# A decode step with attention over a long cache, gated with an MLP: halves of three large loads, P times V's rows summed on DVE, wo in other packets and behind the last V

## The chip, the cores and the metric

The kernel runs on one core of a Trainium2 chip. The core has a matrix engine (PE, with a queue of its own for loading weights, PEld), a vector engine (DVE), a scalar engine (ACT), GpSimd (POOL) and a sync engine (SP), which work side by side and wait for each other by semaphores. PE writes to PSUM, a small accumulation memory; everything else lies in SBUF, 128 partitions. 16 DMA engines move data between HBM and SBUF; a transfer is issued by an instruction on an engine's queue, here almost always SP's, and SP works through its queue in order.

The metric is device time in microseconds, the median of several executions.

## What is computed

Two sequences (B = 2), one new token each. One branch is attention with 32 heads of 128 over a cache of 16384 keys and values per head; the other is a small MLP; a scalar gate mixes them. Cut to what matters:

```python
def reference(A_x, A_k_cache, A_v_cache, A_wq, A_wo, B_x, B_w1, B_w2, B_w3, B_w4, gate_w):
    g = sigmoid((x * gate_w).sum(-1, keepdims=True))        # x = A_x, (2, 1, 1024)
    # attention, H = 32, Dh = 128, Sk = 16384
    q = (x @ wq).reshape(B, 1, H, Dh).transpose(0, 2, 1, 3)
    p = softmax(einsum("bhqd,bhkd->bhqk", q, k_cache) * Dh ** -0.5)
    a = einsum("bhqk,bhkd->bhqd", p, v_cache).transpose(0, 2, 1, 3).reshape(B, 1, H * Dh) @ wo
    # MLP, F = 3584
    h = gelu(layernorm(x) @ w1)
    hs = shift(h) @ w2                # with one token the four shifted quarters are zeros
    x1 = x + hs
    b = x1 + gelu(layernorm(x1) @ w3) @ w4
    return g * a + (1 - g) * b
```

All data are bfloat16. The two caches are 268 MB each, wq and wo 8.4 MB each, w3 and w4 7.3 MB each, w1 and w2 2.1 MB each.

## The kernel before

**Units.** The work on the cache is cut into 32 units: a unit is a pair of heads (`hp`, 16 of them) of one sequence (`b`). Its K is 8.4 MB, 64 KB in each partition: partition p holds 256 consecutive rows of 128 numbers, and the first 64 partitions are one head, the others the second. Its V has the same form.

**Memory.** `mem` has five cells of 32 KB per partition; a K or V takes two. K of even units lies in cells 0 and 1, K of odd units in 1 and 2, so that the next K may start to load when half of the present one has been used (each unit begins with the half that lies in cell 1). V lies in cells 3 and 4, but for unit 30, whose V takes cells 0 and 1 when K is no longer needed there. At the start wq lies in cells 3 and 4, w1 and w2 in cell 2; then w3 and after it w4 take cells 3 and 4, and then the first V.

**A unit n** (the loop at line 567): `score_first` and `score_second` work through K in 8 chunks of 32 rows per partition. DVE transposes a chunk (L425, two buffers), and PE multiplies it by q (L431, 8 products per chunk), which builds the scores S in PSUM. Between the two halves stands the issue of the next K (L97). `softmax_a` transposes S (L452), takes the maximum of each partition (L454) and spreads it on a diagonal (L456, ACT). `softmax_b` has PE bring the maxima together (L462), DVE reduces them (L468), ACT takes the exponentials (L470) with their sums, and a product and a reciprocal give the inverse row sums (L481, L483). P times V of a unit comes two units later: `pv(n - 2)` (L503) makes 64 products into `oacc`, in which 32 rows hold partial results (8 in each of four groups of columns of PE, each with four blocks of 128). `pv_end` scales and copies `oacc` on ACT (L516), and four fp32 products with selecting weights (L521, two records each) add the rows that belong together into O, transposed; L533 multiplies by the gate. After the second sequence of a pair, `wo_project` (L404) multiplies by the pair's two heads of wo: four products of 512 columns into the output sum `arow`, which lies in PSUM in two halves of 512 columns, each in its own group of PE's columns.

**Order.** A scheduler builds each engine's queue nearly in the program's order. SP's queue in a middle unit is: K of the next unit (waits for DVE's transposes of half of this one), V of the unit before (waits for the last P-times-V product that reads cells 3 and 4), and in every fourth unit a load of wo for four heads (`load_wo`, 1 MB, rows of 2 KB, one buffer).

**The MLP** is spread over the first units. `LinearT` (line 197) loads a weight matrix whole and multiplies 128x128 blocks of it by two columns of activations (L217). w3's 224 products run in unit 0 behind S, 56 of them ahead of the softmax's maximum product, 168 behind the product for the row sums; then the gelu follows on DVE and ACT. w4's 224 run in unit 1 in the same way. `lin4.load` waits for the last product that reads w3; `load_v(0)` waits for the last that reads w4. `mlp_post4` starts the output sum with 16 fp32 products (L379).

**The end.** V of unit 31 comes in 11 pieces (`PIECES`, in rows per partition: six of 32, three of 16, two of 8), each issued ahead of its use. The first three go through `pv_moving`; the rows of the others are used as weights against P (L548) as they arrive, into the same sum. Behind V stand two loads of one head of wo each. Then the last `wo_project`, a copy of each half of `arow` (L606 on DVE, L608 on ACT), and one store per half.

## Time and profile before

| | |
|---|---|
| runs of the kernel (us) | 1347.13, 1347.13, 1348.85; median 1347.13 |
| the profiled execution | 1348.32, its span 1346.6 |
| mean granted clock of PE | 0.781 |
| read from HBM | 572.53 MB, 425 GB/s over the span |
| busy, share of the span | PE 59%, DVE 48%, PEld 27%, ACT 9%, POOL 1% |
| largest groups | S products L431 547.9 us, K transposes L425 570.8 us, P times V L503 116.9 us |

The profile is one execution. "Busy" is the time in which an engine had an instruction of that group under way; a matrix product of fp32 has two records. The chain that ended last follows the work back from the last instruction to what released it. A wait is put down to the event that came last. The arrival of a transfer is the moment at which its semaphore was seen; the DMA columns of the windows count its packets, which is earlier. Every line number in a profile line is a line of the kernel it belongs to.

### The profile page before, as it was taken

Reading aid. Unit: us, or ns where it says so; the run is one execution under the profiler, and the core shown is the slowest. Engines: PE = TensorE matmul, PEld = TensorE weight load, DVE = VectorE, ACT = ScalarE, POOL = GpSimd, SP = SyncE. Lnnn points to the kernel's source line nnn. Section 1 sums busy time; section 2 is a strip of 40 time slices with the busy share of each in tenths; the row PEclk is TensorE's granted clock in tenths of the full one; section 3 lists DMA queues with packets and bytes.
Section 4 is the critical chain, followed back from the end, with each engine's and each line's share of the span. In section 5 each row is a group of like instructions: output and inputs, shape, how many; then the busy total and the mean of one; then the engine's idle time right before and its main releaser. Section 6 shows DMA issues by size and latency. Waiting matters only on the chain.

```text
span 1346.6 us, 12381 instructions
## 1 busy us (share of the span) xinstructions
PE 790.9 (59%) x5542; PEld 367.0 (27%) x5542; DVE 644.4 (48%) x503; ACT 127.1 (9%) x197; POOL 15.2 (1%) x54
## 2 busy tenths in 40 slices
PE   2678765554766545566555556655456664555665
PEld 2455322222222222222222222222222222222222
DVE  0434555444555534455554345555344555444450
ACT  0010101111110011110011111001111100111110
POOL 1000000000000000000000000000000000000000
PEclk9967877777887667888777788777778876777886
DMA  9988999999999999999999999999999999999997
GB/s 406 432 368 387 435 436 427 425 429 437 433 431 433 428 439 435 433 433 425 433 433 435 435 435 435 435 432 426 437 437 425 429 433 437 433 433 429 435 435 303
DMA packets 16109, 573.33 MB, mean 426 GB/s; under 512 B 1844, under 2 KB 1848, under 8 KB 6584
## 3 DMA queue, kind: packets, MB, share of 16 engines
q1 hardware_dynamic: 16052, 572.54, 98.8%
q8 instruction: 43, 0.70, 0.2%
q14 instruction: 10, 0.08, 0.0%
q10 hardware_dynamic: 4, 0.00, 0.0%
HBM read 572.53 MB, written 0.00 MB: 425 GB/s over the span
## 4 chain that ended last, share of the span: by engine, by line
DMA 66%; PE 16%; DVE 12%; issue 4%; ACT 0%; another core or an unknown queue 0%; POOL 0%; SPq 0%; DVEq 0%; ACTq 0%
DMA mem<-in_A_k_cache_dram 62%; PE S L431 12%; DVE KT L425 12%; DMA mem<-in_A_v_cache_dram 3%; PE misc L217 3%; DMA xin<-in_A_x_dram 2%; PE misc L248 1%; ACT pt L470 0%; PE arow L379 0%; PE oacc L503 0%; POOL ln_rstd L329 0%; PE misc L462 0%; PE arow L404 0%; PE misc L481 0%
## 5 line engine op out<-in xcount | busy, mean ns | idle before, releaser
L431 PE MATMUL S<-KT,qw 128*128 128x512 bf16 x2048 | 547.9, 418 | 388.4 <-DVE KT L425 388.2
L425 DVE STREAM_TRANSPOSE KT<-mem 128x2048 f32<-128x2048 f32 x256 | 570.8, 2282 | 297.3 <-DMA mem<-in_A_k_cache_dram 245.8
L431 PEld LDWEIGHTS <-qw 128*128 128x128 bf16 x2048 | 219.0, 107 | 712.2 <-issue 533.8
L503 PE MATMUL oacc<-mem,pt 128*8 128x512 bf16 x2008 | 116.9, 386 | 8.7 <-DMA mem<-in_A_v_cache_dram 8.7
L456 ACT ACTIVATE Dm<-ident_s,m 128x128 f32<-128x128 f32 x32 | 12.9, 402 | 1018.4 <-DVE m L454 1018.4
L470 ACT ACTIVATE pt<-St,nb 64x256 bf16<-64x256 f32 x64 | 89.7, 1401 | 58.4 <-DVE nb L468 57.5
L533 DVE TENSOR_SCALAR OT<-misc,g_rep 128x2 bf16<-128x2 f32 x31 | 6.9, 222 | 143.5 <-PE misc L521 143.5
L481 PE MATMUL misc<-rs,lmat 128*128 128x1 f32 x62 | 18.2, 362 | 90.0 <-ACT pt L470 90.0
L503 PEld LDWEIGHTS <-pt 128*8 128x8 bf16 x2008 | 46.7, 87 | 75.7 <-issue 25.3
L452 DVE STREAM_TRANSPOSE St<-S 128x512 f32<-128x512 f32 x32 | 22.9, 717 | 66.2 <-PE S L431 66.2
L483 DVE RECIPROCAL rinv<-misc 128x1 f32<-128x1 f32 x31 | 5.2, 169 | 102.2 <-PE misc L481 102.2
L521 PE MATMUL misc<-sel,osb 128*128 128x2 f32 x256 | 33.7, 254 | 27.1 <-ACT osb L516 27.1
L481 PEld LDWEIGHTS misc<-rs,lmat 128*128 128x128 f32 x62 | 15.5, 311 | 101.2 <-ACT pt L470 101.2
L521 PEld LDWEIGHTS misc<-sel,osb 128*128 128x128 f32 x256 | 31.0, 191 | 43.3 <-ACT osb L516 43.3
L217 PEld LDWEIGHTS <-mem 128*128 128x128 bf16 x576 | 36.3, 170 | 1.8 <-issue 1.4
L470 ACT ACTIVATION_READ_ACCUMULATOR pt<-St,nb 64x1 f32 x64 | 30.5, 477 | 0.0
L516 ACT ACTIVATE osb<-oacc,rinv 128x512 f32<-128x512 f32 x31 | 21.3, 687 | 72.6 <-PE oacc L503 72.6
L248 PE MATMUL misc<-xT,mem 128*128 128x2 bf16 x256 | 7.1, 165 | 26.1 <-DVE xT L243 23.3
L280 POOL TENSOR_TENSOR qw<-qd,mask 128x16 bf16<-128x16 bf16 x32 | 8.4, 265 | 1195.2 <-PE S L431 1166.6
L468 DVE TENSOR_REDUCE nb<-misc 64x1 f32<-64x64 f32 x64 | 14.2, 222 | 5.3 <-PE misc L462 1.3
L224 DVE COPY w_acc<-misc 128x16 f32<-128x16 f32 (+4 forms) x6 | 1.1, 176 | 31.4 <-PE misc L217 31.4
L462 PE MATMUL misc<-Dm,ones_f 128*128 128x128 f32 x64 | 15.8, 331 | 0.0
(83 smaller groups left out, 124.3 us busy)
## 6 DMA issues: line engine op xcount, KB each, us to landing
mem<-in_B_w_dram SPq DMA_DIRECT2D x2, 7168.0 KB, 29.1
wo<-in_A_wo_dram SPq DMA_DIRECT2D x7, 1024.0 KB, 33.0
mem<-in_A_v_cache_dram SPq DMA_DIRECT2D x6, 1024.0 KB, 24.1
mem<-in_B_w_dram SPq DMA_DIRECT2D x2, 2048.0 KB
mem<-in_A_v_cache_dram SPq DMA_DIRECT2D x3, 512.0 KB, 16.7
mem<-in_A_k_cache_dram SPq DMA_DIRECT2D x32, 28.3
wo<-in_A_wo_dram SPq DMA_DIRECT2D x1, 512.0 KB, 32.0
mem<-in_A_v_cache_dram SPq DMA_DIRECT2D x2, 256.0 KB, 13.3
```

What stands on the lines that cost most here:

```text
L217: nc.tensor.matmul(ps[:, c - c0, :], lhsT=wc[:, r, :].rearrange("p (m c) -> p c m", c=self.C)[:, c, :], rhs=self.actT[:, r, :], start=(r = ...
L248: nc.tensor.matmul(qps[:, h, :], lhsT=wq_t[:, r, h * Dh : (h + 1) * Dh], rhs=xT[:, r, :], start=(r == 0), stop=(r == KC - 1),)
L425: nc.vector.transpose(out=kt[:], in_=Kc.rearrange("p j d -> p (j d)").bitcast(FP32))
L431: nc.tensor.matmul(S, lhsT=t[:, v, NG - 1 - m : NG - 1 - m + P], rhs=ktb[:, half * GT : (half + 1) * GT, w, :, e], start=(first and n == 0 ...
L452: nc.vector.transpose(out=st[:].rearrange("p j r -> p (j r)"), in_=S[:])
L462: nc.tensor.matmul(R_ps[:], lhsT=ones_f[:], rhs=Dm[:], start=True, stop=True)
L468: nc.vector.tensor_reduce(out=nb[rows], in_=R_ps[rows, rows], axis=AX.X, op=ALU.min)
L470: nc.scalar.activation(out=Pt[rows, :, e, :].rearrange("p (m a) k -> p a k m", a=GT // 4), in_=st[rows, :, 0:NG].rearrange("p (a k) m -> p ...
L481: nc.tensor.matmul(tot_ps[:, 0:1], lhsT=lmat[:], rhs=rs[:], start=True, stop=True)
L503: nc.tensor.matmul(acc[QP * q : QP * q + 8, :], lhsT=pts[u % NP][:, g].rearrange("p h k -> p (h k)"), rhs=v_view(u)[:, 4 * g : 4 * g + 4, ...
L516: nc.scalar.activation(out=osb[:], in_=oacc[u % 2][:], func=ACTF.Copy, scale=rinvs[u % NP][:, 0:1] if scaled else 1.0,)
L521: nc.tensor.matmul(ot[:], lhsT=osb[:, k * Dh : (k + 1) * Dh], rhs=sel8[:, k : k + 5 : 4], start=(k == 0), stop=(last and k == 3),)
```

## The change

- `LinearT` may load its matrix in parts, each with half of the rows of every partition, in a cell of its own; `compute` works on a part, and the second part's result is added to the first's on DVE. w3 and w4 have two parts (cells 3 and 4). `lin4.load(0)` stands behind the products on the first half of w3, `lin4.load(1)` behind those on the second; the two halves of the first V (`load_v_half`) follow the halves of w4 in the same way.
- `softmax_b` is cut in two; the row sums become `softmax_c`, so that an issue can stand between them.
- `pv_end` and `pv_last`: the rows of `oacc` are weighted by a mask (which carries the inverse row sum and the gate) and added over the four blocks on DVE (`pv_rows`), and one or two fp32 products with a selector of the head replace the four. The ACT copy goes.
- wo is loaded for pairs of heads with rows of 4 KB, two consecutive rows of wo in each partition; O is laid out to fit, even and odd rows apart. The last four heads, not the last two, are loaded one by one behind the last V, and projected at the end.
- The output sum lies in four groups of columns of PE, 256 numbers each, in one tile (cleared once at the start). `wo_project` makes 8 products of 256 columns, `mlp_post4` 32 of 32 columns. At the end DVE copies one half of each group and ACT the other, and there is one store per sequence.
- `PIECES` is seven of 32 and two of 16.

```diff
         nc.sync.dma_start(out=region(v_cell[u], NJ * Dh), in_=cache_rows(A_v_cache, u))
-    PIECES = [32] * 6 + [16] * 3 + [8] * 2
+    def load_v_half(u, k):
+        at = slice(k * CELL, (k + 1) * CELL)
+        nc.sync.dma_start(out=region(v_cell[u], NJ * Dh)[:, at], in_=cache_rows(A_v_cache, u)[:, at])
+    PIECES = [32] * 7 + [16] * 2
     assert sum(PIECES) == NJ
...
     )
+    mask4m = const.tile([P, 4], FP32)
+    nc.vector.tensor_tensor(out=mask4m[:], in0=sel8[:, 0:4], in1=sel8[:, 4:8], op=ALU.add)
+    hsel = const.tile([P, 2], FP32)
+    nc.vector.tensor_reduce(
+        out=hsel[:], in_=sel8[:].rearrange("p (h k) -> p h k", k=4), axis=AX.X, op=ALU.add
+    )
     oacc = [ops.tile([P, 4 * Dh], FP32, name=f"oacc{k}") for k in range(2)]
...
     class LinearT:
-        def __init__(self, W, actT, name, cell, offset):
+        def __init__(self, W, actT, name, cell, offset, nparts=1):
             self.actT = actT
...
             self.C = self.N // P
+            self.rows = self.R // nparts
             self.src = W.rearrange("(p r) n -> p (r n)", p=P)
-            at = cell * CELL + offset
-            self.dst = mem[:, at : at + self.R * self.N]
+            self.at = [(cell + k) * CELL + offset for k in range(nparts)]
             self.acc = mlp.tile([P, self.C, B], FP32, name=f"{name}_acc")
-        def load(self):
-            nc.sync.dma_start(out=self.dst, in_=self.src)
-        def compute(self, c0, c1):
-            wc = self.dst.rearrange("p (r n) -> p r n", n=self.N)
+        def part(self, k):
+            return mem[:, self.at[k] : self.at[k] + self.rows * self.N]
+        def load(self, k=0):
+            n = self.rows * self.N
+            nc.sync.dma_start(out=self.part(k), in_=self.src[:, k * n : (k + 1) * n])
+        def compute(self, k, c0, c1):
+            wc = self.part(k).rearrange("p (r n) -> p r n", n=self.N)
             ps = misc_psum([P, c1 - c0, B])
             for c in range(c0, c1):
-                for r in range(self.R):
+                for r in range(self.rows):
                     nc.tensor.matmul(
...
                         lhsT=wc[:, r, :].rearrange("p (m c) -> p c m", c=self.C)[:, c, :],
-                        rhs=self.actT[:, r, :],
+                        rhs=self.actT[:, k * self.rows + r, :],
                         start=(r == 0),
-                        stop=(r == self.R - 1),
+                        stop=(r == self.rows - 1),
                     )
-            nc.vector.tensor_copy(out=self.acc[:, c0:c1, :], in_=ps[:])
+            acc = self.acc[:, c0:c1, :]
+            if k == 0:
+                nc.vector.tensor_copy(out=acc, in_=ps[:])
+            else:
+                nc.vector.tensor_tensor(out=acc, in0=acc, in1=ps[:], op=ALU.add)
     xn1T = mlp.tile([P, KC, B], BF16)
...
     lin2 = LinearT(B_w2, shT, "w2", 2, KC * D)
-    lin3 = LinearT(B_w3, xn2T, "w3", 3, 0)
-    lin4 = LinearT(B_w4, h2T, "w4", 3, 0)
+    lin3 = LinearT(B_w3, xn2T, "w3", 3, 0, 2)
+    lin4 = LinearT(B_w4, h2T, "w4", 3, 0, 2)
     lin1.load()
...
             )
-    lin3.load()
+    lin3.load(0)
+    lin3.load(1)
     qT = const.tile([P, H, B], BF16)
...
         layernorm_T(x1T[:], xn2T[:], "ln2")
-    NH2 = D // 512
-    arow_t = [rps.tile([QP * k + B, 512], FP32, name=f"arow{k}") for k in range(NH2)]
-    arow = [arow_t[k][QP * k : QP * k + B, :] for k in range(NH2)]
+    NQ = D // Q4
+    arow_t = rps.tile([P, NQ], FP32, name="arow")
+    nc.vector.memset(arow_t[:], 0.0)
+    arow = [arow_t[QP * k : QP * k + B, :] for k in range(Q4)]
     def mlp_post4():
...
         )
-        W = 512 // KC
-        for k in range(NH2):
+        W = NQ // KC
+        for k in range(Q4):
             for c in range(KC):
...
                 )
-    OT = const.tile([P, H, B], BF16)
-    WOH = 4
-    wo_view = A_wo.rearrange("(h d) n -> d h n", d=Dh)
+    OT = const.tile([P, HP, 2, B], BF16)
+    LASTP = 2
+    wo_pairs = A_wo.rearrange("(hp p r) n -> p hp (r n)", p=P, r=2)
+    wo_heads = A_wo.rearrange("(h d) n -> d h n", d=Dh)
     wo_tiles = {}
-    def load_wo(h0, n, step=WOH):
-        t = wopool.tile([P, WOH, D], BF16, name="wo")
-        for k in range(0, n, step):
-            z = min(n, k + step)
-            nc.sync.dma_start(out=t[:, k:z, :], in_=wo_view[:, h0 + k : h0 + z, :])
-        for k in range(n):
-            wo_tiles[h0 + k] = t[:, k, :]
+    def wo_tile(hp0):
+        t = wopool.tile([P, 2, 2, D], BF16, name="wo")
+        for k in range(2):
+            for r in range(2):
+                wo_tiles[hp0 + k, r] = t[:, k, r, :]
+        return t
+    def load_wo_pair(hp0):
+        t = wo_tile(hp0)
+        nc.sync.dma_start(
+            out=t[:].rearrange("p k r n -> p k (r n)"), in_=wo_pairs[:, hp0 : hp0 + 2, :]
+        )
+    def load_wo_last():
+        t = wo_tile(HP - LASTP)
+        for k in range(2):
+            for r in range(2):
+                nc.sync.dma_start(out=t[:, k, r, :], in_=wo_heads[:, H - 4 + 2 * k + r, :])
     def wo_project(hp):
-        for h in (2 * hp, 2 * hp + 1):
-            for k in range(NH2):
+        for r in range(2):
+            for k in range(Q4):
                 nc.tensor.matmul(
                     arow[k],
-                    lhsT=OT[:, h, :],
-                    rhs=wo_tiles[h][:, k * 512 : (k + 1) * 512],
+                    lhsT=OT[:, hp, r, :],
+                    rhs=wo_tiles[hp, r][:, k * NQ : (k + 1) * NQ],
                     start=False,
-                    stop=(h == H - 1),
+                    stop=(hp == HP - 1 and r == 1),
                     skip_group_check=True,
...
         rs_tiles[u] = rs
+    def softmax_c(u):
+        rs = rs_tiles.pop(u)
         tot_ps = misc_psum([P, 2])
...
         pv_moving(u, 0, NJ // 4, NJ // 4)
-    def pv_sum(u, ot, scaled, last):
-        osb = ppool.tile([P, 4 * Dh], FP32, name="osb")
-        nc.scalar.activation(
-            out=osb[:], in_=oacc[u % 2][:], func=ACTF.Copy,
-            scale=rinvs[u % NP][:, 0:1] if scaled else 1.0,
-        )
-        for k in range(4):
-            nc.tensor.matmul(
-                ot[:],
-                lhsT=osb[:, k * Dh : (k + 1) * Dh],
-                rhs=sel8[:, k : k + 5 : 4],
-                start=(k == 0),
-                stop=(last and k == 3),
-            )
+    def pv_rows(u, mask):
+        acc = oacc[u % 2]
+        part = ppool.tile([P, Dh], FP32, name="part")
+        red = ppool.tile([P, 2, Dh], FP32, name="red")
+        nc.vector.tensor_scalar(
+            out=part[:], in0=acc[:, 0:Dh], scalar1=mask[:, 0:1], scalar2=None, op0=ALU.mult
+        )
+        for k in range(1, 4):
+            in0 = acc[:, k * Dh : (k + 1) * Dh]
+            twice = k == 3
+            nc.vector.scalar_tensor_tensor(
+                out=red[:] if twice else part[:],
+                in0=in0.unsqueeze(1).to_broadcast([P, 2, Dh]) if twice else in0,
+                scalar=mask[:, k : k + 1],
+                in1=part[:].unsqueeze(1).to_broadcast([P, 2, Dh]) if twice else part[:],
+                op0=ALU.mult,
+                op1=ALU.add,
+            )
+        return red[:].rearrange("p e d -> p (e d)")
     def pv_end(u):
         hp, b = units[u]
-        ot = misc_psum([P, 2])
-        pv_sum(u, ot, True, True)
+        mask = stat.tile([P, 4], FP32, name="maskr")
         nc.vector.tensor_scalar(
-            out=OT[:, 2 * hp : 2 * hp + 2, b], in0=ot[:], scalar1=g_rep[:, b : b + 1],
-            scalar2=None, op0=ALU.mult,
-        )
+            out=mask[:], in0=mask4m[:], scalar1=rinvs[u % NP][:, 0:1],
+            scalar2=g_rep[:, b : b + 1], op0=ALU.mult, op1=ALU.mult,
+        )
+        red = pv_rows(u, mask)
+        if hp >= HP - LASTP:
+            ot = misc_psum([P, 2])
+            nc.tensor.matmul(ot[:], lhsT=red[:, 0:Dh], rhs=hsel[:], start=True, stop=True)
+            nc.vector.tensor_copy(out=OT[:, hp, :, b], in_=ot[:])
+            return
+        ot = misc_psum([P, 2, 2])
+        for r in range(2):
+            nc.tensor.matmul(
+                ot[:, r, :],
+                lhsT=red[:, r : 2 * Dh : 2],
+                rhs=hsel[:],
+                start=True,
+                stop=True,
+            )
+        for e in range(2):
+            rows = slice(e * HALF, (e + 1) * HALF)
+            nc.vector.tensor_copy(out=OT[rows, hp, :, b], in_=ot[rows, :, e])
         if b == B - 1:
...
         pv_moving(u, 0, moving, moving)
-        pv_sum(u, ot, False, False)
+        red = pv_rows(u, mask4m)
+        nc.tensor.matmul(ot[:], lhsT=red[:, 0:Dh], rhs=hsel[:], start=True, stop=False)
         V = v_view(u)
...
             )
-        nc.vector.tensor_tensor(
-            out=OT[:, 2 * hp : 2 * hp + 2, b], in0=ot[:], in1=rinvs[u % NP][:], op=ALU.mult
-        )
-        wo_project(hp)
+        nc.vector.tensor_tensor(out=OT[:, hp, :, b], in0=ot[:], in1=rinvs[u % NP][:], op=ALU.mult)
+        for k in range(HP - LASTP, HP):
+            wo_project(k)
     compute_gate()
     layernorm_T(xT[:], xn1T[:], "ln1")
-    lin1.compute(0, lin1.C)
+    lin1.compute(0, 0, lin1.C)
     mlp_post1()
-    lin2.compute(0, lin2.C)
+    lin2.compute(0, 0, lin2.C)
     mlp_post2()
...
         if n == 0:
-            lin3.compute(0, FC // 4)
+            load_wo_pair(0)
+            lin3.compute(0, 0, FC // 2)
             softmax_b(n)
-            lin3.compute(FC // 4, FC)
+            lin3.compute(0, FC // 2, FC)
+            lin4.load(0)
+            softmax_c(n)
+            lin3.compute(1, 0, FC)
+            lin4.load(1)
             gelu_T(lin3.acc[:], h2T[:], FC)
-            load_wo(0, WOH)
-            lin4.load()
         elif n == 1:
-            lin4.compute(0, KC // 4)
+            lin4.compute(0, 0, KC // 2)
             softmax_b(n)
-            lin4.compute(KC // 4, KC)
+            lin4.compute(0, KC // 2, KC)
+            load_v_half(0, 0)
+            softmax_c(n)
+            lin4.compute(1, 0, KC)
+            load_v_half(0, 1)
             mlp_post4()
-            load_v(0)
         else:
...
             if n == NU - 1:
-                load_wo(H - 2, 2, 1)
+                load_wo_last()
             softmax_b(n)
-        if n % 4 == 1 and n > 1:
-            load_wo(n - 1, min(WOH, H - 2 - (n - 1)))
+            softmax_c(n)
+        if n % 4 == 1 and 1 < n < NU - 3:
+            load_wo_pair((n - 1) // 2)
     pv(NU - 2)
...
     pv_last(NU - 1)
-    out_row = mlp.tile([QP + B, 512], BF16)
-    rows = out.rearrange("b s d -> (b s) d")
-    nc.vector.tensor_copy(out=out_row[0:B, :], in_=arow[0])
-    nc.sync.dma_start(out=rows[:, 0:512], in_=out_row[0:B, :])
-    nc.scalar.activation(out=out_row[QP : QP + B, :], in_=arow[1], func=ACTF.Copy)
-    nc.scalar.dma_start(out=rows[:, 512:1024], in_=out_row[QP : QP + B, :])
+    out_row = mlp.tile([P, NQ], BF16)
+    used = slice(0, QP * (Q4 - 1) + B)
+    half = NQ // 2
+    nc.vector.tensor_copy(out=out_row[used, 0:half], in_=arow_t[used, 0:half])
+    nc.scalar.activation(out=out_row[used, half:NQ], in_=arow_t[used, half:NQ], func=ACTF.Copy)
+    for b, queue in ((0, nc.sync), (1, nc.scalar)):
+        queue.dma_start(
+            out=out[b, 0].rearrange("(k n) -> k n", k=Q4),
+            in_=out_row[b : b + QP * (Q4 - 1) + 1 : QP, :],
+        )
 # ---- launch: one core; inputs and outputs as the reference has them ----
```

## The prediction

> **What bounds the kernel now.** I read the page first: the 40 slices and the chain that ended last.
>
> ```profile
> span 1346.6 us, 12381 instructions
> ...
> DMA  9988999999999999999999999999999999999997
> GB/s 406 432 368 387 435 436 427 425 429 437 433 431 433 428 439 435 433 433 425 433 433 435 435 435 435 435 432 426 437 437 425 429 433 437 433 433 429 435 435 303
> ...
> DMA 66%; PE 16%; DVE 12%; issue 4%; ACT 0%; another core or an unknown queue 0%; POOL 0%; SPq 0%; DVEq 0%; ACTq 0%
> ```
>
> The transfers bound it: nearly every slice moves about 433 GB/s, and no compute engine is busy for more than 59% of the span. Only three places fall short: slices 3 and 4 (67 to 135 us), and the last. So the second view is the busy time in windows of 5 us (columns: window, length, PE, PEld, DVE, ACT, POOL busy, granted clock, DMA share, GB/s).
>
> ```profile
> 85.00:90.00 5.00, 5.00 (x82) 5.00 (x81) 0.00 (x0) 0.00 (x0) 0.00 (x0) 0.50 0.90 370
> 90.00:95.00 5.00, 3.75 (x60) 3.69 (x59) 0.83 (x4) 0.25 (x1) 0.00 (x0) 0.50 0.62 202
> 95.00:100.00 5.00, 2.25 (x6) 0.85 (x6) 4.82 (x4) 0.00 (x1) 0.00 (x0) 0.50 0.78 333
> ...
> 130.00:135.00 5.00, 4.48 (x75) 4.40 (x74) 0.41 (x3) 0.00 (x0) 0.00 (x0) 0.50 0.11 43
> ```
>
> Two holes, around 92 us and around 133 us. The waits of the DMA queue on SP say what ends them (queue and line, what it waited for: total us, times, longest).
>
> ```profile
> SPq L210 <- PE misc L217: 23.3, 1, 23.3
> SPq L100 <- PE misc L217: 19.7, 1, 19.7
> ```
>
> w4 (L210) waits for the last matmul that reads w3, since both lie in cells 3 and 4; the first V (L100) waits in the same way for the last one that reads w4. The chain gives the times: the last 168 matmuls of each product, and the arrival of K of unit 3 (start, length, what).
>
> ```profile
> 83.13 10.64 PE misc L217 x168
> ...
> 124.40 10.10 PE misc L217 x168
> ...
> 145.39 31.85 DMA mem<-in_A_k_cache_dram
> 177.26 2.32 DVE KT L425
> ```
>
> **How much the holes cost.** From unit 5 on, K arrives every 38.70 us (215.98 to 254.68 in the chain) for one K and one V, 16.78 MB: 433.5 GB/s. K of unit 0 arrives at 53.49 with 20.97 MB before and in it, 48.4 us of stream, so 5.1 us lie around the stream. I put 2.1 of them ahead of it (the first issue ends at 1.2, and after the issues of w4 at 93.78 and of V at 134.51 the bytes move about 1 us later) and 3.0 behind (arrival after the end of the stream). K of unit 3 closes 70.26 MB; without holes it would arrive at 5.1 + 162.1 = 167.2, and it arrives at 177.26: 10.1 us are lost. By place: the stream through the first wo (37.75 MB) ends at 89.2 and w4 begins at 94.8, a hole of 5.6; K of unit 2 then ends at 131.1 and V begins at 135.5, a hole of 4.4. Sum 10.0.
>
> **Halves of w3, w4 and V.** Each half is released by its own matmuls: 112 for a half of w3 or w4, where 224 released all of it. The built program's order on PE says where they stand: after four of a unit's eight K chunks come 31 of the first 56, after the fifth chunk the other 25; the second 56 follow the softmax's maximum product, the 112 of the second half the row-sum product. One such matmul takes 63 ns (10.64 / 168), a chunk of S 1.9 us. Unit 0: chunk 4 ends at 66.4, and with 3.5 us of product pushed in between, S ends at 77.9 (75.2 before). St 0.72, m 0.42, Dm 0.40, the product of 0.78 and their hand-overs bring it to 80.6; 56 matmuls, 3.5, to 84.2: the first half of w4 is issued there, not at 93.78. Row sum 0.6 and 112 matmuls, 7.1: second half at 92.0. The adds and the gelu (1.7, as before) let K of unit 1 begin on DVE at 93.7 (95.40 before), and K of unit 2 is issued 10.5 later as before (105.90), at 104.2. Unit 1 likewise: S begins at 96.0, takes the 18.9 of before plus 3.5 of product less 0.9 that fits into PE's pauses of 0.29 per chunk, ends at 117.5, and 2.7 + 3.5 later, at 123.7, the first half of V is issued (134.51 before), at 131.5 the second, and K of unit 2 begins on DVE at 132.3 (135.03 before), which issues K of unit 3 at 142.7 (145.39).
>
> The stream without holes needs these to move at 89.2, 97.6, 106.1, 125.5, 135.1 and 144.8 (8.47 us for half a w4, 19.35 for a K, half that for half a V). With 1 us after issue they can at 85.2, 93.0, 105.2, 124.7, 132.5 and 143.7. All six are in time, but three by only 0.9, 0.8 and 1.1 us. One thing pushes the last: the 16 fp32 products that start the output row (L379, 32 records in 3.1 us, 97 ns each for 64 columns) become 32 of half the width. By columns they cost 3.1 again, by records 6.2, which makes K of unit 3 late by 2.0; I take 4.2, about no margin. For all three thin margins I leave 1.0 us of hole. Ends: everything won, 10.1; each of the three releases late by 1.5 beyond its margin, 5.5. Gain taken: 9.0.
>
> New waits: PE's queue now holds the second half of each unit's S behind a half of w3 (arrives 61.9, PE there at 66.4), of w4 (100.7 against 108.3) and of V (138 against about 145). The SP queue gains three issues of 0.33 to 0.4 us, each behind a wait that ends earlier than the old one. K of the next unit is released by the first four chunks, which stand ahead of these waits.
>
> A rule that speaks against halves: the Trainium skill, "DMA: Bandwidth & Descriptors", section "Anatomy of one DMA — SWDGE (gpsimd) path", gives every DMA a fixed 2.0 us on top of its bytes, and its "Rules for kernel authors" ask for 1 MiB or more. Taken as stream time, three more DMAs would return 6 us, leaving 3.7. The trace shows queued transfers differently: the last pieces of V, 0.5 MB each, are used at 1336.72, 1337.93, 1339.16, about 1.22 us apart, which is their bytes at 430 GB/s, so nothing is charged for the cut while others are queued. I go by the row.
>
> **P times V summed on DVE.** Removed per unit: an ACT copy (687 ns) and 8 fp32 records on PE (1.05 us). Added on DVE: three operations of 128x128, one of 128x256, a small mask and one copy more. Nearest rows: 225 ns (128x64 out of PSUM) and 228 (128x128 in SBUF) below, 886 (128x128, L129) above; so 1.4 to 5.0 us per unit, I take 1.9. What hides it, in a middle unit (start, length, engine, what; idle before in brackets):
>
> ```profile
> 303.88 0.33 SPq L97 DMA_DIRECT2D mem<-in_A_k_cache_dram  x1
> ...
> 318.19 0.33 SPq L100 DMA_DIRECT2D mem<-in_A_v_cache_dram  x1
> ...
> 334.64 4.50 DVE L425 STREAM_TRANSPOSE KT<-mem 128x2048 f32<-128x2048 f32 x2 [10.29 <-DMA mem<-in_A_k_cache_dram]
> ```
>
> DVE sits idle for 10.29 us before the next K arrives, and V was issued before the sum begins. Behind the sum on DVE wait only the softmax's minima and then that K. Cost 0. If the cover went, each unit would pay; even then K's issue has spare: the stream through its V ends at 331.6 + 19.35 = 350.9, and K is issued 10.5 after the arrival, at 345.1, and moves at 346.1: 4.8 us early.
>
> **wo in 4 KB packets.** A unit with four heads of wo takes 41.26 us between arrivals (293.38 to 334.64), one without 38.70: 2.56 for 1.05 MB, against 2.42 at the stream's rate. Seven such loads: 1.0 at most is there to win, and a loss of the same size isn't excluded. I take 0.4.
>
> **Last heads behind V, and the output.** The bytes are the same, so the last arrival stands where it stood, 1342.9 (wo's second issue at 1334.2 plus 8.7). Now:
>
> ```profile
> 1342.33 1.20 PE L404 MATMUL arow<-wo,OT 128*2 128x512 bf16 x4 [0.25 <-DVE OT L555]
> ...
> 1343.56 0.68 DVE L606 CAST out_row<-arow 2x512 bf16<-2x512 f32 x1 [1.29 <-PE arow L404]
> 1343.60 0.59 ACT L608 ACTIVATE out_row<-arow 2x512 bf16<-2x512 f32 x1 [11.79 <-PE arow L404]
> ...
> 1344.27 0.33 SPq L607 DMA_DIRECT2D out_dram<-out_row  x1
> ```
>
> The second pair of wo products begins at 1342.94, on the arrival of wo; it takes 0.6, the two copies 0.7 side by side. After the change four products of 256 columns remain, in four column groups: about 0.3. The copies shrink to 128 columns (0.28 on DVE; ACT about 0.3, 402 ns for 128 columns in its L456 row), but ACT waits for DVE in the built program, so 0.6. That wins 0.3 to 0.4. The cut at the end (two pieces of 0.5 MB for three and two of 0.25, four wo of 0.25 MB for two) can move the last arrival by one piece, 0.6 us, either way, and V's end now comes 1.2 earlier against it. Taken 0.3, ends -1 and +1.5.
>
> **Sum.** 9.0 + 0.4 + 0.3 = 9.7: span 1346.6 to 1336.9. The profiled execution took 1348.32 (1.72 around the span), which gives 1338.6; it lies 1.2 above the median of the three runs, 1347.13, and on that scale the forecast is 1337.4.
>
> **Rivals.**
> - *The thin margins fail.* The releases of K (unit 2), V and K (unit 3) come 1.5 us later than worked out. For it: PE ran at a granted 0.50 in both holes, so anything added to PE there is dear; against it: the products' 63 ns are from just that clock. Gain 5.5 + 0.7: 1341.
> - *The halves don't release early.* A half of w4 would still have to wait for all of w3. Against it: the built program's wait of each half names PE and the arrival of its own half. Then 1346.5, no change that a measurement of this kernel can tell (0.2%, 2.7 us).
> - *DVE takes over (slower).* The sums become part of the way from V's arrival to the next K. It decides when they outgrow DVE's idle 10.29 and then the 4.8 spare of K's issue, 15.1 us per unit; at 17 us per unit, 30 units pay 1.9 each, 57 us, less 9.7: 1394. Against it: my upper price is 5.0.
>
> **How the numbers follow.** Forecast 0.73, thin margins 0.14, no early release 0.04, DVE or another unforeseen cost 0.06, more than worked out (a shorter tail, wo) 0.03. The forecast's own range is 1334.5 to 1340: 10.1 + 1.0 + 1.5 won at the best, 7 at the worst. To leave out no more than 2 in 10, with 1 us for the runs' own spread, I take 1334 to 1342.5. Faster 0.88, within 0.2% 0.05, slower 0.07.
>
> **What would show it.** Slices 3 and 4 at about 430 GB/s; w4's halves issued near 84 and 92, V's near 124 and 131.5; K of unit 3 used at 167 to 169; K arrivals still 38.7 apart; DVE's idle time before K near 9.5 in a middle unit; the last products four of 256 columns after wo. Wrong would be: SP still waiting long for L217's successor, intervals above 38.8, or a last wo that arrives later than the shifted 1342.9.

## The result, and the profile after

The changed kernel takes 1341.28 us (median of 5 runs, 1341.09 to 1341.38), the kernel before 1347.13 (1347.06 to 1349.07) beside it on the same chip: a ratio of 0.9951, with a 95% interval of 0.9936 to 0.9966. That is 5.9 us faster where 9.7 were forecast; the time lies inside the range, near its slow end. The profiled executions differ by more: spans of 1346.6 and 1339.4, 7.2 us. The kernel before spreads over 2 us from run to run, and its profiled execution, 1348.32, lies in the upper part; in the three later comparisons its median was 1347.74, 1347.65 and 1348.05.

The page of the changed kernel, its first lines and its chain:

```profile
span 1339.4 us, 12490 instructions
...
DMA  9999999999999999999999999999999999999997
GB/s 406 425 429 432 440 431 433 435 423 440 429 435 437 429 429 437 425 435 435 435 431 429 429 437 431 429 427 430 440 431 431 427 433 423 437 435 435 433 423 309
...
DMA 67%; PE 16%; DVE 12%; issue 4%; ACT 0%; another core or an unknown queue 0%; POOL 0%; SPq 0%; ACTq 0%; DVEq 0%
```

Slices 3 and 4, 368 and 387 GB/s before, are at 429 and 432; behind the first slice, only the last is still low. The windows where the holes were (the columns are those of the windows before):

```profile
90.00:95.00 5.00, 0.99 (x15) 0.88 (x14) 3.68 (x8) 0.25 (x1) 0.00 (x0) 0.50 1.10 469
95.00:100.00 5.00, 5.00 (x16) 1.78 (x15) 3.53 (x2) 0.00 (x0) 0.00 (x0) 0.63 1.01 436
...
130.00:135.00 5.00, 5.00 (x68) 3.32 (x66) 4.33 (x3) 0.00 (x0) 0.00 (x0) 0.72 1.02 436
```

At 90 to 100 us, 202 and 333 GB/s have become 469 and 436; at 130 to 135, 43 has become 436. The DMA queue's waits on SP, and the chain at K of unit 3:

```profile
SPq L226 <- PE misc L233: 25.1, 2, 18.0
SPq L104 <- PE misc L233: 24.9, 2, 17.9
```

```profile
138.97 30.07 DMA mem<-in_A_k_cache_dram
169.05 2.32 DVE KT L462
```

The issues of the three transfers that had thin margins, K of unit 2, the first half of V and K of unit 3 (what, times; shortest, median and longest in ns; first and last start in us):

```profile
L97 SPq DMA_DIRECT2D mem<-in_A_k_cache_dram x1: 328/328/328, 103.0 to 103.0; - x1
L104 SPq DMA_DIRECT2D mem<-in_A_v_cache_dram x1: 327/327/327, 121.3 to 121.3; - x1
L97 SPq DMA_DIRECT2D mem<-in_A_k_cache_dram x1: 327/327/327, 139.0 to 139.0; - x1
```

SP still waits about 25 us in total for the products of w3 and of w4, now in two waits each; the waits simply end while an earlier transfer is under way. K of unit 3, used at 177.26 before, is used at 169.05: 8.2 us are won there. K of unit 31, the last, is used at 1272.93 instead of 1281.67.

The end:

```profile
1335.42 0.38 PE L441 MATMUL arow<-wo,OT 128*2 128x256 bf16 x4 [0.26 <-DMA wo<-in_A_wo_dram]
...
1335.86 0.29 DVE L677 CAST out_row<-arow 98x128 bf16<-98x128 f32 x1 [2.27 <-PE arow L441]
1336.18 0.28 ACT L678 ACTIVATE out_row<-arow 98x128 bf16<-98x128 f32 x1 [32.82 <-DVE out_row L677]
1336.49 0.65 SPq L680 DMA_DIRECT2D out_dram<-out_row  x1
1336.49 1.35 ACTq L680 DMA_DIRECT2D out_dram<-out_row  x1
```

The last four products stand directly behind the arrival of wo and take 0.44 with their hand-over, the copies 0.63 one after the other, and from the issue of the stores to the end of the span it is 2.9 us.

### The profile page after: what moved, and what is told of

Its sections match the earlier page's. It is cut to its first block, busy times and chain, and to the rows that moved or that the text cites. A ratio compares the mean times of both kernels' runs of the same rounds, so it can differ in the third digit from the quotient of the medians.

```text
span 1339.4 us, 12490 instructions
## 1 busy us (share of the span) xinstructions
PE 768.8 (57%) x5502; PEld 351.9 (26%) x5502; DVE 705.1 (53%) x695; ACT 105.2 (8%) x165; POOL 15.2 (1%) x54
## 4 chain that ended last, share of the span: by engine, by line
DMA 67%; PE 16%; DVE 12%; issue 4%; ACT 0%; another core or an unknown queue 0%; POOL 0%; SPq 0%; ACTq 0%; DVEq 0%
DMA mem<-in_A_k_cache_dram 62%; PE S L468 12%; DVE KT L462 12%; PE misc L233 2%; DMA mem<-in_A_v_cache_dram 2%; DMA xin<-in_A_x_dram 2%; DMA wo<-in_A_wo_dram 1%; PE misc L268 1%; ACT pt L507 0%; PE arow L402 0%; PE oacc L543 0%; DVE St L489 0%; POOL ln_rstd L350 0%; PE misc L344 0%
## 5 line engine op out<-in xcount | busy, mean ns | idle before, releaser
L559 DVE TENSOR_SCALAR part<-oacc,maskr 128x128 f32<-128x128 f32 x31 | 10.9, 351 | 83.0 <-PE oacc L543 83.0
L590 PE MATMUL misc<-hsel,red 128*128 128x2 f32 x112 | 17.5, 261 | 51.5 <-DVE red L565 51.5
L590 PEld LDWEIGHTS misc<-hsel,red 128*128 128x128 f32 x112 | 15.9, 202 | 64.8 <-issue 62.6
L565 DVE SCALAR_TENSOR_TENSOR part<-oacc,maskr,part 128x128 f32<-128x128 f32 x62 | 21.8, 351 | 2.2
L599 DVE CAST OT<-misc 64x2 bf16<-64x2 f32 x56 | 9.0, 160 | 22.9 <-PE misc L590 22.6
```

Source lines behind the costliest of these rows:

```text
L565: nc.vector.scalar_tensor_tensor(out=red[:] if twice else part[:], in0=in0.unsqueeze(1).to_broadcast([P, 2, Dh]) if twice else in0, scalar ...
L590: nc.tensor.matmul(ot[:, r, :], lhsT=red[:, r : 2 * Dh : 2], rhs=hsel[:], start=True, stop=True,)
```

## The experiments

Each of ten kernels was timed in five rounds against the kernel before. The changed kernel itself was not timed again beside them, so a difference to it also holds what moved the median of the kernel before from 1347.13 to between 1347.65 and 1348.05. The measure that tells most is the distance between two uses of K by consecutive units, read from the first transposes of each unit: 38.70 with one K and one V in it ("plain"), more where a load of wo is among them ("wo interval").

### The halves alone

The kernel before, with `LinearT`, `softmax_c` and `load_v_half` of the change, and its loop in units 0 and 1:

```diff
+    lin3 = LinearT(B_w3, xn2T, "w3", 3, 0, 2)
+    lin4 = LinearT(B_w4, h2T, "w4", 3, 0, 2)
...
+            load_wo(0, WOH)
+            lin3.compute(0, 0, FC // 2)
...
+            lin4.load(0)
...
+            load_v_half(0, 0)
```

> The kernel before with only the halves of w3, w4 and the first V (the sum on ACT and PE, wo in rows of 2 KB, the output sum in two groups and the pieces of before stay). Theory A, that the two holes are the gain and the rest of the change costs about 1.3 us (wo 0.1 us in each of seven loads, the end 0.3 to 0.6): K of unit 3 is used near 169.1, the profiled span is 1338 to 1339, the median 1340 to 1341, not above the whole change. Theory B, that a good part of the gain comes from the other parts: K of unit 3 near 169.1 or later and a median of 1343 or more. Theory C, that the halves would win more alone, because the output sum's 64 records no longer stand in PE's way: K of unit 3 near 167.2.

Measured: 1339.92 us (1339.67 to 1340.26), ratio 0.9945 (0.9932 to 0.9957), span 1338.4; K of unit 3 at 169.23; plain intervals 38.70, wo intervals 41.15 to 41.19. The halves are more than the whole gain: by the medians, the rest of the change together costs 1.4 us. Theory A holds, B falls, and so does C: K of unit 3 isn't earlier although the 64 records of the output sum were 32 again.

### The change without the halves

```diff
-    lin3 = LinearT(B_w3, xn2T, "w3", 3, 0, 2)
-    lin4 = LinearT(B_w4, h2T, "w4", 3, 0, 2)
+    lin3 = LinearT(B_w3, xn2T, "w3", 3, 0)
+    lin4 = LinearT(B_w4, h2T, "w4", 3, 0)
...
-            load_v_half(0, 0)
...
-            load_v_half(0, 1)
             mlp_post4()
+            load_v(0)
```

> The changed kernel with w3, w4 and the first V loaded whole again, everything else of the change kept. Theory A: K of unit 3 comes back to 177.3, two holes near 92 and 133 us, and the median lies 0.3 to 1.5 us above the kernel before (1347.4 to 1348.6). Theory B: 1345 or less.

Measured: 1348.49 us (1347.58 to 1349.66) against 1347.74, ratio 1.0007 (0.9999 to 1.0016). Its windows have the holes back, and SP's single long waits with them:

```profile
90.00:95.00 5.00, 3.31 (x53) 3.25 (x52) 1.21 (x7) 0.25 (x1) 0.00 (x0) 0.50 0.65 215
...
130.00:135.00 5.00, 4.32 (x74) 4.23 (x74) 1.19 (x4) 0.00 (x0) 0.00 (x0) 0.50 0.54 187
```

K of unit 3 is used at 176.15, 1.1 before the 177.26 of the kernel before, the median 0.8 above it. So the holes are the gain, from both sides.

### The sum on DVE alone

The kernel before, with `mask4m`, `hsel`, `pv_rows` and the mask in `pv_end` of the change:

```diff
-        pv_sum(u, ot, True, True)
+        red = pv_rows(u, mask)
+        nc.tensor.matmul(ot[:], lhsT=red[:, 0:Dh], rhs=hsel[:], start=True, stop=True)
```

> The kernel before with only P times V's rows summed on DVE. Theory A (hidden in DVE's idle time before K): K arrivals stay 38.7 apart, the median within 0.5 us of the kernel before. Rival (DVE's sum gets on the path to the next K): intervals above 38.8 and 1.9 us for each of 30 units, up to 1400; a small part of it would show as 1349 or more.

Measured: 1348.97 us (1348.63 to 1349.71) against 1347.74, ratio 1.001 (1.0002 to 1.0019). Slower by 1.2, but not in the way of the rival: plain intervals stay 38.70, and DVE still idles 6.4 to 11.1 us before each K from unit 3 on. Only the wo intervals grew, from 41.18 to 41.41 (one of the six has 42.43; it holds a part of the longer interval near unit 10, which is explained further down). Theory A's time was missed, and neither theory had a reason for this.

### wo in rows of 2 KB

```diff
-            out=t[:].rearrange("p k r n -> p k (r n)"), in_=wo_pairs[:, hp0 : hp0 + 2, :]
+            out=t[:].rearrange("p k r n -> p (k r) n"), in_=wo_heads[:, 2 * hp0 : 2 * hp0 + 4, :]
```

> The changed kernel with wo loaded by heads, rows of 2 KB as before, one load for four heads; O is laid out for it, so that each unit has one selecting product and one copy instead of two. Theory A (rows of 4 KB cost): the interval between K arrivals with a wo load falls from 41.3 to 41.2, the span by 0.5 to 0.8 us, median 1340.5 to 1340.8. The prediction's step (rows of 4 KB win): intervals of 41.4 and 0.4 us more, 1341.7.

Measured: 1342.29 us (1342.03 to 1342.49), 1.0 above the changed kernel; wo intervals of 41.39 to 41.63, where the changed kernel has 41.24 to 41.45. Theory A was wrong and the prediction's step nearer: rows of 4 KB do win here. But then the wo intervals of the changed kernel should have been below those of the kernel before, and they are above. Both runs show the same excess in every kernel that sums on DVE, whatever the rows of wo.

### The place of wo's buffer

What these kernels share, beside the sum, are its small constant tiles, which stand ahead of wo's buffer in the allocation: it moves from 207104 bytes (a multiple of 256) to 207168 (64 past one). The buffers of K and V stand ahead of them and don't move. The next two kernels change only that place, with an unused tile that GpSimd clears once at the start. It also shifts the other buffers behind it, those of the K transposes among them; wo's is the only one of these that a load from HBM writes in the middle units. The kernel before:

```diff
+    gap64 = const.tile([P, 16], FP32)
+    nc.gpsimd.memset(gap64[:], 0.0)
     oacc = [ops.tile([P, 4 * Dh], FP32, name=f"oacc{k}") for k in range(2)]
```

> The kernel before with one unused tile of 64 bytes per partition among the constants, so that wo's buffer begins at 207168 instead of 207104 (as it does in every kernel with the sum on DVE); nothing else differs. Theory D, that wo's place in SBUF makes its loads slower: the intervals between K arrivals with a wo load rise from 41.18 to 41.4, the others stay 38.70, the span rises by 1.2 to 1.7 us. Rival, that the sum on DVE itself disturbs the wo load: intervals stay 41.18 and the time that of the kernel before.

The changed kernel:

```diff
+    gap192 = const.tile([P, 48], FP32)
+    nc.gpsimd.memset(gap192[:], 0.0)
     oacc = [ops.tile([P, 4 * Dh], FP32, name=f"oacc{k}") for k in range(2)]
```

> The changed kernel with one unused tile of 192 bytes per partition, which puts wo's buffer at 207360, a multiple of 512. Theory D: the wo intervals fall from 41.26 to 41.45 to 41.0 to 41.2, the span by 1 to 2 us, median 1339.5 to 1340.3. Rival (the DVE sum is the cause): no change, 1341.3.

Measured: the kernel before with 64 unused bytes takes 1348.81 us against 1347.65 (ratio 1.0011, 1.0002 to 1.002), with no other work in it but the clearing of the tile; the changed kernel with 192 unused bytes takes 1340.16 (1339.82 to 1340.34), 1.1 less than without. One wo interval in each, from DVE's timeline, the first transposes of units 6 and 7 (start, length, what; idle before). The kernel before, unit 6 (unit 7 starts at 334.64, as shown further up):

```profile
293.38 4.50 DVE L425 STREAM_TRANSPOSE KT<-mem 128x2048 f32<-128x2048 f32 x2 [7.18 <-DMA mem<-in_A_k_cache_dram]
```

The kernel before with 64 bytes:

```profile
292.15 4.50 DVE L427 STREAM_TRANSPOSE KT<-mem 128x2048 f32<-128x2048 f32 x2 [7.62 <-DMA mem<-in_A_k_cache_dram]
333.67 4.50 DVE L427 STREAM_TRANSPOSE KT<-mem 128x2048 f32<-128x2048 f32 x2 [10.55 <-DMA mem<-in_A_k_cache_dram]
```

The changed kernel as it is, and then with 192 bytes:

```profile
285.32 4.51 DVE L462 STREAM_TRANSPOSE KT<-mem 128x2048 f32<-128x2048 f32 x2 [6.99 <-DMA mem<-in_A_k_cache_dram]
326.70 4.50 DVE L462 STREAM_TRANSPOSE KT<-mem 128x2048 f32<-128x2048 f32 x2 [8.92 <-DMA mem<-in_A_k_cache_dram]
```

```profile
285.13 4.50 DVE L464 STREAM_TRANSPOSE KT<-mem 128x2048 f32<-128x2048 f32 x2 [6.95 <-DMA mem<-in_A_k_cache_dram]
326.25 4.50 DVE L464 STREAM_TRANSPOSE KT<-mem 128x2048 f32<-128x2048 f32 x2 [8.73 <-DMA mem<-in_A_k_cache_dram]
```

The differences of the two starts are what to read: 41.26, 41.52, 41.38 and 41.12. Over the six wo intervals of each kernel: 41.17 to 41.26 in the kernel before, 41.41 to 41.64 with the 64 bytes; 41.24 to 41.45 in the changed kernel, 41.12 to 41.16 with the 192. The last is with the DVE sum in place, and its plain intervals from unit 5 on are 38.69 to 38.72, so the sum itself costs the transfers nothing. Theory D holds. The trace's single packets agree: one of 2 KB takes 84.4 ns on average in the kernel before and 86.9 with the 64 bytes, one of 4 KB 162.4 in the changed kernel and 159.5 with the 192. It also settles the rows: off the multiple, 4 KB rows save about 0.15 per load (41.24 to 41.45 against 41.39 to 41.63); on it, 4 KB rows (41.12 to 41.16) and 2 KB rows (the halves alone, 41.15 to 41.19) are the same to 0.03.

### The place of K and V

The halves alone, and two unused tiles:

```diff
+    gap384 = const.tile([P, 96], FP32)
+    nc.gpsimd.memset(gap384[:], 0.0)
     mem = const.tile([P, 5 * CELL], BF16, name="mem")
...
+    gap128 = const.tile([P, 32], FP32)
+    nc.gpsimd.memset(gap128[:], 0.0)
     oacc = [ops.tile([P, 4 * Dh], FP32, name=f"oacc{k}") for k in range(2)]
```

> The kernel with the halves alone, with unused tiles that put the five cells of K and V at a multiple of 512 (16896 instead of 16512, which is 128 above one) and leave wo where it stood against 512. If a place off such a multiple cost K and V what it costs wo, the plain interval of 38.70 would fall, by up to 0.15 (16.78 MB at 435 GB/s are 38.57), and the span by up to 4 us, to 1335. If only rows of a few KB feel it: 38.70 and 1339.9 as before.

Measured: 1337.76 us (1337.58 to 1337.9), 2.2 below the halves alone; ratio 0.9927 (0.9913 to 0.9941). The uses of K by units 4 and 5, first in the halves alone, then with the cells moved:

```profile
207.93 4.51 DVE L439 STREAM_TRANSPOSE KT<-mem 128x2048 f32<-128x2048 f32 x2 [7.69 <-DMA mem<-in_A_k_cache_dram]
246.65 4.50 DVE L439 STREAM_TRANSPOSE KT<-mem 128x2048 f32<-128x2048 f32 x2 [8.15 <-DMA mem<-in_A_k_cache_dram]
```

```profile
207.22 4.50 DVE L443 STREAM_TRANSPOSE KT<-mem 128x2048 f32<-128x2048 f32 x2 [7.16 <-DMA mem<-in_A_k_cache_dram]
245.81 4.50 DVE L443 STREAM_TRANSPOSE KT<-mem 128x2048 f32<-128x2048 f32 x2 [7.63 <-DMA mem<-in_A_k_cache_dram]
```

These are 38.72 and 38.59 apart. Over all units the plain interval falls from 38.70 to values between 38.59 and 38.82, a third of them at 38.59 to 38.61. Single packets of 64 KB agree: 2418.0 ns on average against 2420.4, those lengthened by other work left out. So the large rows of K and V feel their place too, by up to 0.11 in 38.70. Of the 2.4 us between the two profiled spans, 0.75 are there at unit 3, 1.1 come between units 3 and 30, and the rest at the end.

The kernel before, with the same two:

```diff
+    gap384 = const.tile([P, 96], FP32)
+    nc.gpsimd.memset(gap384[:], 0.0)
     mem = const.tile([P, 5 * CELL], BF16, name="mem")
...
+    gap128 = const.tile([P, 32], FP32)
+    nc.gpsimd.memset(gap128[:], 0.0)
     oacc = [ops.tile([P, 4 * Dh], FP32, name=f"oacc{k}") for k in range(2)]
```

> The kernel before with nothing changed but the place of the cells (16896; wo where it stood against 512). If the place wins by itself: 2.0 to 2.7 us, 1345.2 to 1345.6, plain intervals of 38.6 to 38.7, the two holes as before. If the stream only gains where it has no holes: 1347.5.

Measured: 1346.45 us (1344.41 to 1347.07) against 1348.05, ratio 0.9986 (0.9977 to 0.9995); plain intervals 38.58 to 38.77; K of unit 3 at 177.17, so the holes are as they were. The gain is there without the halves, 1.6 at the median, a little under what was expected, in runs that spread over 2.7 us.

### The stores

The changed kernel with the 192 bytes, and another end:

```diff
+    rows = out.rearrange("b s d -> (b s) d")
...
-    nc.vector.tensor_copy(out=out_row[used, 0:half], in_=arow_t[used, 0:half])
-    nc.scalar.activation(out=out_row[used, half:NQ], in_=arow_t[used, half:NQ], func=ACTF.Copy)
-    for b, queue in ((0, nc.sync), (1, nc.scalar)):
-        queue.dma_start(
-            out=out[b, 0].rearrange("(k n) -> k n", k=Q4),
-            in_=out_row[b : b + QP * (Q4 - 1) + 1 : QP, :],
-        )
+    nc.vector.tensor_copy(out=out_row[used, :], in_=arow_t[used, :])
+    for k in range(Q4):
+        queue = nc.sync if k % 2 == 0 else nc.scalar
+        queue.dma_start(out=rows[:, k * NQ : (k + 1) * NQ], in_=out_row[QP * k : QP * k + B, :])
```

> The changed kernel with the same 192 bytes, and at the end one DVE copy of all 256 columns (no ACT copy behind it) and four stores of two rows, two on SP and two on ACT, in place of the two stores with four separate partitions each. From the last wo arrival to the end the changed kernel took 4.0 us (products 0.44, copies 0.63, stores 2.9). If the store's form is what costs: 3.3 to 3.6, the span 0.4 to 0.7 below that of the padded kernel. If it is the number of pieces: no change.

Measured: 1339.50 us (1339.21 to 1339.63), 0.7 below the padded kernel. The end of it:

```profile
1334.44 0.38 PE L443 MATMUL arow<-wo,OT 128*2 128x256 bf16 x4 [0.23 <-DMA wo<-in_A_wo_dram]
1334.88 0.42 DVE L679 CAST out_row<-arow 98x256 bf16<-98x256 f32 x1 [2.13 <-PE arow L443]
1335.33 0.62 SPq L682 DMA_DIRECT2D out_dram<-out_row  x2
1335.33 0.82 ACTq L682 DMA_DIRECT2D out_dram<-out_row  x2
```

One copy of 0.42 replaces two of 0.63 in a row, and the two issues on ACT's queue take 0.82 together where one of four scattered partitions took 1.35. From the last wo to the end of the span (1337.8) it is 3.4 us, not 4.0. Both were changed at once; by the two timelines the single copy saves about 0.2 and the stores, from their issue to the end of the span, 0.4 (2.9 to 2.5).

### All of it

The changed kernel with the four stores, and both buffers on a multiple of 512:

```diff
+    gap384 = const.tile([P, 96], FP32)
+    nc.gpsimd.memset(gap384[:], 0.0)
     mem = const.tile([P, 5 * CELL], BF16, name="mem")
...
+    gap320 = const.tile([P, 80], FP32)
+    nc.gpsimd.memset(gap320[:], 0.0)
     oacc = [ops.tile([P, 4 * Dh], FP32, name=f"oacc{k}") for k in range(2)]
```

> The changed kernel with both buffers at a multiple of 512 (the cells at 16896, wo at 207872) and the four stores behind one DVE copy. If the three gains add: 2.2 us of the cells' place on top of 1339.5, so 1337.3; plain intervals of 38.6 to 38.7, wo intervals near 41.1. If the place of the cells won by something else in the kernel with the halves alone: 1339.5.

Measured: 1336.85 us (1336.69 to 1337.06), ratio 0.9918 (0.9904 to 0.9931), span 1335.3. It is faster than both kernels: 4.4 us below the changed one. Measured apart, the three gains are 1.1 for wo's place, 2.2 for that of the cells and 0.7 for the end, together 3.9, so they add.

## Why the prediction was right or wrong, point by point

- **The holes (gain 9.0, ends 5.5 and 10.1).** Right in mechanism: shown by the halves alone and by the change without them. Right in place: all six releases came, none later than worked out. The halves of w4 were issued at 83.3 and 90.9 (worked out 84.2 and 92.0), K of unit 2 at 103.0 (104.2), V's halves at 121.3 and 128.8 (123.7 and 131.5), K of unit 3 at 139.0 (142.7). The 64 narrow fp32 records took 2.87, not 4.2, at the same granted 0.50 as the 32 before (3.11): the price went by columns. So no late release used up the 1.0 that was held back. Still the gain was 8.2, not 10.1; that it lies near the 9.0 taken is partly luck, since the 1.0 was set aside for something else. The step that failed is "without holes it would arrive at 167.2". K of unit 2 arrived at 129.0 (103.0 and 26.0 to landing), 0.5 behind the stream's sum (128.5); the 16.78 MB behind it took 40.05, not 38.70.
- **What the stream's sum left out: loads of instructions.** Such intervals of 39.9 to 40.3 come three more times in this kernel, at units 10, 17 and 25, and three times in the kernel before (10, 18 and 25). The trace says why. Beside the transfers it has a queue named "instruction", with 16 KB packets, about one per unit. In the changed kernel between 129 and 169 us (packets, MB, share of 16 engines):

```profile
q1 hardware_dynamic: 427, 17.40, 100.9%
q8 instruction: 2, 0.03, 0.3%
```

Linked end to start, the trace's packets form 16 chains, one for each DMA engine. From the end of K of unit 2 to the end of K of unit 3, 14 of these engines took 38.75 to 38.78 us for their share of the 16.78 MB; the other two took 40.31, and two 16 KB packets lie in that stretch, at 131.4 and 150.1. So one such packet holds its engine up by 1.5 us. A K is used about 0.5 us after its last engine has finished: one of the two delayed engines had been among the last at K of unit 2 and finished K of unit 3 at 168.59, alone, 1.3 behind the next one, and DVE began at 169.05. The long intervals of the kernel before read the same way where the chains can be followed: at unit 10 the last engine took 40.25, the undelayed ones 38.69 to 38.72. At unit 9, with a plain interval of 38.75, a delayed engine took 40.19, but it had been 1.4 ahead of the last. So the halves don't make these intervals; a delay shows in K's arrival when it falls on an engine that is already among the last. The holes hid some of it: behind the second one, all 16 engines began V within 0.6 us (135.48 to 136.03), while without it they lie 2.1 apart at the end of K of unit 2 and go straight on. No run here takes the instruction loads away.
- **A fixed cost per transfer.** The Trainium skill, "DMA: Bandwidth & Descriptors", section "Anatomy of one DMA — SWDGE (gpsimd) path", sets 2.0 us on each DMA beside its bytes; its fit is for transfers issued from GpSimd, and these are issued from SP. By it, three DMAs more would have cost 6 us of the holes' 10. The gain at K of unit 3 was 8.2, and 1.35 of the missing 1.9 are the interval just explained. No run here shows the 2.0 charged on a queue that has transfers waiting.
- **The sum on DVE (cost 0).** Right, but for a reason that wasn't in the sum. Its operations took 351 ns for 128x128 and 484 for 128x256, with the mask 1.8 us per unit, and 0.1 more for the copies (1.9 taken); DVE's idle time before K of unit 7 fell from 10.29 to 8.92. With wo's buffer put back on a multiple, the plain intervals are 38.69 to 38.72, as in the halves alone. What it did cost, 1.2 us over the kernel before, came from its constants, which pushed wo's buffer 64 bytes on: 64 unused bytes cost the same.
- **wo in 4 KB rows (gain 0.4).** Wrong in sign as the change stands: K's lead over the kernel before shrinks from 8.21 us at unit 3 to 7.49 at unit 30, as much as the six wo intervals grew together (0.7). Two things were wrong. The row it was read from, 41.26, is the longest of the six wo intervals of the kernel before; the others are 41.17 to 41.19, so all seven loads together had about 0.5 to win, not 1.0. And the place of the buffer, which the change moved by 64 bytes, was not in the sum; it cost more than the rows could bring. On a multiple of 256 the rows make no difference that shows.
- **The end (gain 0.3).** Wrong by 0.6. The last wo arrives within 0.1 of where the step put it: 61.3 us after the last K before, 62.5 after the change, of which 1.24 are the two heads that no longer stand ahead of that K (39.93 against 38.69 in the interval before it). Products and copies became shorter by about 0.2 and 0.1, as said. The term that failed is the stores, which the sum left as they were: from their issue to the end of the span it was 2.3 before, and two stores of four scattered partitions take 2.9. Span after last K: 64.9 before, 66.5 less 1.24 now, a loss of 0.3.
- **The sum and its scale.** By terms in the profiled executions: 9.0 became 8.2, 0.4 became a loss of 0.7, 0.3 a loss of 0.3: 9.7 became 7.2. The rest to the 5.9 of the medians is the step "it lies 1.2 above the median": the changed kernel's profiled execution lies 0.2 below its own, so the difference of medians is 1.4 smaller than that of the two profiles. Against the later medians of the kernel before, 1347.7 to 1348.1, the changed kernel gains 6.4 to 6.8.
- **The rivals.** The thin margins did not fail: their 1341 came out, but by luck, with every release early. The halves did release early, and DVE never came near K: from unit 3 on it had 6.1 us left at the least.

## What to carry to other kernels

In a kernel bound by its transfers, look for the few windows in which they stop, find the one wait behind each on the issuing queue, and cut the buffer so that its first half is released while an earlier transfer is still under way; that was worth more than everything else in this change, and cutting a queued transfer in two cost nothing that showed. A load has arrived when the slowest of the 16 engines has finished its share, so work that falls on one engine alone can delay all of it. After any change to small tiles, look at where the large buffers that transfers write to have moved: 64 bytes cost 1.2 us here, three times what the wider rows of wo were hoped to bring. And read a gain against the spread of the kernel before, not against one profile of it.

## What the runs showed of the hardware that was not expected

- The place in SBUF of the buffer that a transfer writes to sets its speed a little. A 1 MB load of wo costs about 0.23 us more at 64 bytes past a multiple of 256 than on one (41.41 to 41.64 against 41.17 to 41.26, nothing else changed). The 64 KB rows of K and V at 128 past a multiple of 512 take 38.70 per 16.78 MB, on the multiple often 38.59 to 38.61; that was worth 2.2 us in the kernel with the halves. Which multiple it takes, 256 or 512 or something between, was not separated.
- A 16 KB load of instructions, about one per unit, takes one of the 16 DMA engines about 1.5 us (40.25 to 40.31 for its share of 16.78 MB, where an engine without one took 38.69 to 38.78). In most of the kernels it shows three or four times, near units 10, 17 or 18 and 25 and, without the holes, at unit 3, as an interval that is 1.0 to 1.6 us longer (in a few kernels spread over two); elsewhere it hides, as at unit 9 of the kernel before, on an engine that is ahead of the last.
- A store from four partitions 32 apart took 1.35 us to issue on ACT's queue, and 0.65 on SP's; two stores from two neighbouring partitions each took 0.82 and 0.62 together.
